# Hash bits on four column quarters and small placing transfers, in place of divisor sums on four column quarters, in an attention and feed-forward kernel

## The chip, the cores and the metric

The kernel runs on one core of a Trainium2 chip. The metric is device time in microseconds (us) of one execution. A core has engines that run side by side, each working through its own instructions in order: TensorE (PE, matrix products; PEld is its loading of weights), VectorE (DVE), ScalarE (ACT), GpSimd (POOL), and SyncE (SP), which here only issues DMA transfers. An instruction waits on semaphores until the work it needs is done; whatever stands behind it in the same queue waits too.

## The reference

Two stages. The first is attention with a hash mask, for 4 batches of 8 heads, 768 tokens, head size 64; the second is a feed-forward block on 3072 tokens of width 512 with 2048 hidden units.

```python
q_bits = (np.einsum('bhsd,dk->bhsk', q, proj) > 0)     # proj: 64 x 6
k_bits = (np.einsum('bhsd,dk->bhsk', k, proj) > 0)
q_bucket = np.sum(q_bits * powers, axis=-1)            # k_bucket alike
mask = q_bucket[:, :, :, None] == k_bucket[:, :, None, :]
scores = np.where(mask, scale * np.matmul(q, k.transpose(0, 1, 3, 2)), -1e9)
attn = softmax(scores)
out = np.matmul(attn, v)                               # to (B*S, H*D) = x
h = x @ w_in
g = h * erf(log1p(exp(h)))                             # a stable form of it
return g @ w_out
```

## The kernel before

**Attention.** Heads are taken two at a time: 16 pairs, heads a and b of a pair on partitions 0-63 and 64-127. A pair's 768 queries are cut into two halves of 384. So there are 32 half-pairs, numbered h, and half-pair h belongs to pair h // 2. For a half-pair, `score` (L529) computes six blocks of 128 keys x 384 queries for both heads into a PSUM tile `st`; the PSUM pool for such tiles (`big`) has three buffers. Each block takes two products: one in bf16 of the hash bits `kb` and `qb`, which adds a huge negative number wherever two buckets differ, and one in f32 of `k` and `q`. `exponential` (ACT, L543) takes the block to `e_all`, which holds nine blocks. `weigh` (L602) multiplies with `v` into `av`; `leave` (ACT, L659) copies `av` to the tile `x`, of which there are two buffers, one per pair.

**The hash bits.** `bits_of` (L358) multiplies q and k with `proj_sb` (128 x 64: six columns per head and zeros) for both halves of queries. `q` goes to partitions 0-63 and `k` to 64-127 of the PSUM tile, so two products run side by side on two column halves of the PE array. `sign_of` (ACT, L371) takes the sign of all 768 columns, `weigh_bits` (DVE, L382, once per head) multiplies the key's bits with weights into `kb`, `copy_bits` (DVE, L392) repeats the query's bits on partitions 64-127.

**The divisor.** `sum_keys` (DVE, L590) adds the six blocks of a half-pair in three or four instructions, most of them two blocks wide, in the memory of `x_sum` and of a block `x1` that the feed-forward part uses later. `divisor` (PE, L635) sums over the partitions with a 128 x 32 tile of ones, in four products of 192 columns on the four column quarters. `keep_divisor` (ACT, L648) copies the result to `z`. Per pair a chain through DRAM follows: `spread` (L678, `z` to `zd`), `gather` (L685, `zd` to `zc`, 12 numbers on each of 128 partitions), `invert` (DVE, L695 and L698), `ungather` (L703, to `rd`), `widen` (L713, two transfers, `rd` to `r` on all partitions), `normalise` (DVE, L721, `x` times `r`), and `send` (L727, `x` to `xs` in DRAM). `leave` of pair i writes the buffer of `x` that `send` of pair i-2 reads.

**Beside it.** `start_pair` issues the six loads of q, k and v (L342, L347; three sets of buffers). `measure` (ACT, L620) sums squares of q and k for a check of bounds. The 32 pieces of `w_in` and `w_out`, given as 64-bit floats, are fetched by POOL (L439) and turned to f32 by ACT (L453, L460) and DVE (L467 to L515); `presum_weights` (DVE, L742) makes sums of them.

**Order.** PE's order is written out by hand in `order`: after the first score, per half-pair h the scores of the next two quarters of work, then for even h the bits of the next pair, then the divisor of half-pair h-1, then the two `weigh`. All other instructions are placed by `arrange`, a list planner with a cost and a rank for each operation; it fixes the order on each engine, and the chip keeps to it. All transfers of the chain and all loads stand in one queue, SP's.

**Feed-forward.** The rest (L1098, L1238 on PE; L1116 to L1195 on ACT and DVE) uses Strassen-like sums of blocks, and is ordered by the same planner.

Of the kernel before, what the change touches and what calls it, by code (L numbers as in the profile page):

```python
# [63 lines left out]
P = 128  # L64
# [129 lines left out]
def kernel(  # L194
# [35 lines left out]
    QR = 32  # L230
    WARM = 7
    proj_sb = const.tile([P, 2 * QR], F32, name="proj_sb")
    weight = const.tile([P, 2], F32, name="weight")
    ones = const.tile([P, D], F32, name="ones")
# [23 lines left out]
    steps = const.tile([P, 5], F32, name="steps")  # L258
    for c, (end, factor) in enumerate(
        (  # L260
            (NBIT, NBIT + 1.0),
            (NBIT + 1, -float(NBIT)),
            (QR, -1.0),
            (QR + NBIT, NBIT + 1.0),
            (QR + NBIT + 1, -float(NBIT)),
        )
    ):
        nc.vector.tensor_scalar(
            out=steps[:, c : c + 1],
            in0=row,  # L270
            scalar1=float(end),
            scalar2=factor * BIG,
            op0=ALU.is_lt,
            op1=ALU.mult,
        )
    nc.vector.reduce_sum(out=weight[:, 0:1], in_=steps[:, 0:2], axis=AX.X)
    nc.vector.reduce_sum(out=weight[:, 1:2], in_=steps[:, 2:5], axis=AX.X)
    nc.vector.memset(sgn, -(2.0**-27))
# [87 lines left out]
    def sign_bits(d, bitp, cols):  # L366

        if cols.start == 0:
            for what in ("qb", "kb"):
                d[what] = bitp.tile([P, S], BF16, name=what, tag=what)  # L370
# [23 lines left out]
    def take_bits(d, bitp, halves=(0, 1)):  # L394
        cols = slice(halves[0] * HS, (halves[-1] + 1) * HS)
        sign_bits(d, bitp, cols)
# [4 lines left out]
    def attention():  # L401
        NS = NPAIR * 4
        with (
            tc.tile_pool(name="load", bufs=3) as load,
            tc.tile_pool(name="bitp", bufs=2) as bitp,
# [8 lines left out]
            def big(name):  # L414
                return psum.tile([P, 2, 512], F32, name=name, tag="big", bufs=3)

            junk = ep.tile([P, HS], BF16, name="junk")
            NE = 3 * GC
            e_all = ep.tile([P, NE, 2, HS + 1], F32, name="e_all")
            nc.vector.memset(e_all[:, :, :, HS : HS + 1], 1.0)  # L420
            pairs = {}
            raws = {}
            NH = NPAIR * 2
            wide_sums = [
                t.rearrange("p a b c -> p (a b c)")[:, 0 : 4 * HS].rearrange(
                    "p (n a c) -> p n a c", n=2, a=2
                )
                for t in (x_sum[:, :, :, :], blocks[1][:, :, :].rearrange("p k (a t) -> p k a t", a=2))
            ]
# [107 lines left out]
            def block(n, c):  # L537
                return e_all[:, (n * GC + c) % NE, :, :]
# [8 lines left out]
            def sum_steps(h):  # L547

                at = [(2 * h * GC + k) % NE for k in range(2 * GC)]
                if h >= NH - 2:
                    return [((0, 1), (0, 1), (1, 1), 0)] + [((k,), "s0", (k, 1), 0) for k in range(2, 6)]
                if at[3] == at[2] + 1:
                    return [
                        ((0, 1, 2, 3), (0, 2), (2, 2), 2),
                        ((4, 5), "s2", (4, 2), 2),
                        ((), "s0", "s1", 0),
                    ]
                return [  # L560
                    ((0, 1, 3, 4), (0, 2), (3, 2), 2),
                    ((2,), "s0", (2, 1), 0),
                    ((5,), "s1", (5, 1), 1),
                    ((), "s0", "s1", 0),
                ]

            def last_sum(h):
                return len(sum_steps(h)) - 1 if h >= 0 else 0

            def sum_keys(h, k):  # L570
                i, half = divmod(h, 2)
                d = pairs[i]
                if k == 0:
                    if h >= NH - 2:
                        d["sum", half] = sums.tile([P, 1, 2, HS], F32, name="sum", tag="sum")
                    else:
                        d["sum", half] = wide_sums[h % 2]
                s = d["sum", half]
                _, one, two, where = sum_steps(h)[k]

                def term(what):
                    if isinstance(what, str):
                        n = int(what[1])
                        return s[:, 0:2, :, :] if n == 2 else s[:, n : n + 1, :, :]
                    first, count = what
                    first = (2 * h * GC + first) % NE
                    return e_all[:, first : first + count, :, 0:HS]

                into = s[:, 0:2, :, :] if where == 2 else s[:, where : where + 1, :, :]
                nc.vector.tensor_tensor(out=into, in0=term(one), in1=term(two), op=ALU.add)  # L590
# [26 lines left out]
            def measure(i, n, half):  # L617
# [3 lines left out]
                    out=junk,  # L621
# [5 lines left out]
            def divisor(h):  # L627


                i, half = divmod(h, 2)  # L630
                d = pairs[i]
                z = d["z_ps"] = bank("z_ps")[:, 0 : HS // 2]
                for n in range(4):
                    ab, part = divmod(n, 2)
                    nc.tensor.matmul(  # L635
                        out=z[n * QR : (n + 1) * QR, :],
                        lhsT=ones[:, 0:QR],
                        rhs=d["sum", half][:, 0, ab, part * HS // 2 : (part + 1) * HS // 2],
# [3 lines left out]

            def keep_divisor(h):
                i, half = divmod(h, 2)
                d = pairs[i]
                if half == 0:
                    d["z"] = home(i, "z")
                nc.scalar.copy(  # L648
                    out=d["z"][:, half * HS // 2 : (half + 1) * HS // 2], in_=d.pop("z_ps")
                )  # L650
# [22 lines left out]
            def spread(i):  # L673

                d = pairs[i]
                zd = d["zd"] = dram.tile([2, 4, HS // 2], F32, name="zd", tag="zd")
                d["zc"] = small.tile([P, 2 * S // P], F32, name="zc", tag="zc")
                nc.sync.dma_start(  # L678
# [1000 lines left out]
```

## Time and profile before

| | us |
|---|---|
| median of three runs | 933.58 (931.9 to 934.86) |
| the profiled execution, its own time | 934.86 |
| its span, first to last instruction | 932.9 |
| attention, from the first score to the first product of the feed-forward part | 9.65 to 339.4 |
| PE busy in that stretch of 329.75 us | 325.91 |
| DVE, ACT busy in it | 300.17, 256.07 |
| PE busy after 339.4, in 593.5 us | 583.63 |

Between the profiled execution's own time and its span lie 2 us outside the instructions. Engine times are busy times; idle time of an engine costs something only where another engine waits for it in the end. The granted clock of PE is 0.997 of full speed.

### The profile page before, as it was taken

Reading aid. Unit: us, or ns where it says so; the run is one execution under the profiler, and the core shown is the slowest. Engines: PE = TensorE matmul, PEld = TensorE weight load, DVE = VectorE, ACT = ScalarE, POOL = GpSimd, SP = SyncE. Lnnn points to the kernel's source line nnn. Section 1 sums busy time; section 2 is a strip of 40 time slices with the busy share of each in tenths; the row PEclk is TensorE's granted clock in tenths of the full one; section 3 lists DMA queues with packets and bytes.
Section 4 is the critical chain, followed back from the end, with each engine's and each line's share of the span. In section 5 each row is a group of like instructions: output and inputs, shape, how many; then the busy total and the mean of one; then the engine's idle time right before and its main releaser. Section 6 shows DMA issues by size and latency. Waiting matters only on the chain.

```text
span 932.9 us, 12993 instructions
## 1 busy us (share of the span) xinstructions
PE 916.8 (98%) x5003; PEld 661.9 (71%) x5003; DVE 829.7 (89%) x1041; ACT 771.0 (83%) x1002; POOL 17.4 (2%) x35
## 2 busy tenths in 40 slices
PE   8999999999999999999999999999999999999996
PEld 3444444444444458888888888888888888888885
DVE  4999998999888997899999889998899789988995
ACT  5888787768876838999998998899989997899891
POOL 0000000000000000000000000000000000000000
PEclk9999999999999999999999999999999999999998
DMA  8365455576654322010212012210221111001211
GB/s 198 99 158 147 132 148 139 147 200 165 147 149 131 97 103 97 1 46 34 80 68 79 34 46 69 80 34 34 79 78 36 34 65 49 34 34 46 68 35 48
DMA packets 61398, 80.92 MB, mean 87 GB/s; under 512 B 33296, under 2 KB 46224, under 8 KB 61328
## 3 DMA queue, kind: packets, MB, share of 16 engines
q1 hardware_dynamic: 56672, 64.08, 23.9%
q0 software_dynamic: 4352, 15.73, 5.6%
q8 instruction: 41, 0.67, 0.3%
q10 hardware_dynamic: 304, 0.20, 0.1%
q14 instruction: 29, 0.24, 0.1%
HBM read 64.07 MB, written 15.93 MB: 86 GB/s over the span
## 4 chain that ended last, share of the span: by engine, by line
PE 85%; DVE 7%; DMA 4%; ACT 2%; issue 1%; SPq 0%; DVEq 0%; ACTq 0%
PE M L1238 30%; PE X L1098 27%; PE st L529 11%; PE av L602 9%; PE M L1098 3%; PE bits L358 2%; DMA xs<-x 1%; ACT e_all L543 1%; DVE x_sum L590 1%; PE z_ps L635 1%; DVE x L590 1%; DMA zd<-z 1%; DMA zc<-zd 1%; DVE x L721 1%; DMA r<-rd 1%
## 5 line engine op out<-in xcount | busy, mean ns | idle before, releaser
L1165 DVE SCALAR_TENSOR_TENSOR e<-w,e 128x1024 f32<-128x1024 f32 x144 | 173.4, 1221 | 5.8 <-ACT w L1161 3.0
L1161 ACT ACTIVATE w<-w,cq 128x1024 f32<-128x1024 f32 x144 | 160.7, 1143 | 1.9
L543 ACT ACTIVATE e_all<-st 128x768 f32<-128x768 f32 x192 | 149.1, 819 | 11.3 <-PE st L529 11.3
L529 PE MATMUL st<-q,k 64*128 64x384 f32 x768 | 156.6, 486 | 0.0
L1238 PE MATMUL M<-w_out_sb,h 128*128 128x256 f32 x576 | 140.2, 380 | 0.4 <-DVE h L1180 0.4
L602 PE MATMUL av<-e_all,v 128*64 128x385 f32 (+1 forms) x768 | 131.1, 490 | 0.0
L1098 PE MATMUL X<-x,w_in_sb 128*128 128x256 f32 x512 | 121.2, 380 | 0.0
L1238 PEld LDWEIGHTS M<-w_out_sb,h 128*128 128x128 f32 x576 | 109.3, 190 | 15.9 <-DVE h L1180 1.1
L1098 PEld LDWEIGHTS X<-x,w_in_sb 128*128 128x128 f32 x512 | 97.1, 190 | 13.8 <-ACT h L1116 0.6
L602 PEld LDWEIGHTS av<-e_all,v 128*64 128x64 f32 x768 | 52.4, 136 | 67.2 <-issue 65.4
L1238 PE MATMUL M<-wt,S 128*128 128x256 f32 x384 | 93.4, 379 | 0.4 <-DVE S L1195 0.4
L529 PEld LDWEIGHTS st<-q,k 64*128 64x128 f32 x768 | 69.1, 190 | 32.8 <-issue 32.1
L1098 PE MATMUL X<-x_sum,w_sum 128*128 128x256 f32 x344 | 81.7, 380 | 1.8 <-ACT h L1116 1.8
L1238 PEld LDWEIGHTS M<-wt,S 128*128 128x128 f32 x384 | 72.9, 190 | 10.7 <-DVE S L1195 0.8
L1098 PEld LDWEIGHTS X<-x_sum,w_sum 128*128 128x128 f32 x344 | 65.1, 190 | 12.0 <-ACT h L1116 3.3
L1116 ACT COPY h<-X 128x512 f32<-128x512 f32 x85 | 49.0, 577 | 22.3 <-PE X L1098 21.4
L1142 DVE SCALAR_TENSOR_TENSOR w<-w,e 128x1024 f32<-128x1024 f32 x48 | 58.4, 1221 | 9.6 <-ACT w L1137 9.3
L529 PE MATMUL st<-qb,kb 64*128 64x384 bf16 x384 | 63.7, 327 | 3.3 <-ACT e_all L543 3.2
L1180 DVE TENSOR_TENSOR h<-h,e 128x1024 f32<-128x1024 f32 x48 | 58.0, 1221 | 6.1 <-ACT e L1176 5.9
L659 ACT COPY x<-av 128x384 f32<-128x384 f32 x32 | 15.3, 478 | 57.4 <-DMA xs<-x 28.8
L1156 ACT ACTIVATE w<-e 128x1024 f32<-128x1024 f32 x48 | 50.4, 1050 | 13.3 <-DVE e L1152 13.0
L1152 DVE TENSOR_TENSOR e<-e,w 128x1024 f32<-128x1024 f32 x48 | 57.5, 1219 | 2.7 <-ACT e L1148 2.6
(117 smaller groups left out, 1421.0 us busy)
## 6 DMA issues: line engine op xcount, KB each, us to landing
wt<-wt SPq DMA_DIRECT2D x24, 768.0 KB, 4.3
raw<-in_w_out_dram POOLq DMA_DIRECT2D x16, 512.0 KB, 3.9
raw<-in_w_in_dram POOLq DMA_DIRECT2D x14, 512.0 KB, 4.2
v<-in_v_dram SPq DMA_DIRECT2D x32, 192.0 KB, 4.5
xs<-x SPq DMA_DIRECT2D x16, 384.0 KB, 2.4
q<-in_qkT_dram SPq DMA_DIRECT2D x30, 192.0 KB, 3.4
k<-in_qkT_dram SPq DMA_DIRECT2D x30, 192.0 KB, 4.2
r<-rd SPq DMA_DIRECT2D x30, 192.0 KB, 3.5
```

The source lines that it names most:

```text
L529: nc.tensor.matmul(out=st[:, ab, 0:HS], lhsT=d["k" + src][rows, keys], rhs=d["q" + src][rows, cols], start=(part == 0), stop=(part == 1),)
L543: nc.scalar.activation(out=e[:, :, 0:HS], in_=st[:, :, 0:HS], func=AF.Exp, scale=scale)
L602: nc.tensor.matmul(out=d["av"][rows, 0:w], lhsT=d["v"][:, g * GC + c, rows], rhs=e[:, ab, 0:w], start=(g == 0 and c == 0), stop=(g == 1 an ...
L1098: nc.tensor.matmul(out=d[where][:, u, :], lhsT=a[:, kc, f : f + P], rhs=b[:, kc, :], start=(first and u == 0 and kc == 0), stop=(last and ...
L1116: nc.scalar.copy(out=quarter(p, q), in_=st[p][where])
L1142: nc.vector.scalar_tensor_tensor(out=w, in0=w, scalar=-1.0, in1=st[p]["e", v], op0=ALU.add, op1=ALU.subtract)
L1152: nc.vector.tensor_tensor(out=s, in0=s, in1=st[p].pop(("w", v)), op=ALU.subtract)
L1156: nc.scalar.activation(out=z, in_=st[p]["s", v], func=AF.Square)
L1161: nc.scalar.activation(out=q, in_=z, func=AF.Square, bias=cq[:, j : j + 1])
L1165: nc.vector.scalar_tensor_tensor(out=s, in0=st[p].pop(("q", v, j)), scalar=ERF_Q[j][1], in1=s, op0=ALU.add, op1=ALU.mult,)
L1180: nc.vector.tensor_tensor(out=h, in0=h, in1=st[p].pop(("s", v)), op=ALU.mult)
L1238: nc.tensor.matmul(out=banks[name][:, sub, :], lhsT=a[:, u, sub * P : (sub + 1) * P], rhs=b[:, u, :], start=(c == 0 and k == 0), stop=(c = ...
```

## The change

Pairs 1 to 15 get their hash bits in another way; pair 0 keeps the old one. `bits_of` now multiplies with `proj_q` (128 x 32, head a in columns 0-5, head b in 16-21), and q and k of both halves of queries go to four column quarters of one PSUM bank. One `sign_of` of 384 columns makes a bf16 tile `sg` of them, one `weigh_bits` weighs the key's rows in place, and `place_bits` issues eight DMA transfers on SP, each of 7 rows of 384 bf16 numbers, from `sg` to the rows of `qb` and `kb` where they belong. Those two tiles exist twice (`spare`), filled with zeros by POOL beforehand; the set that pair 0 has used is cleared by `clean`. The bits of a pair come earlier in PE's order: pair 1's after the second quarter of scores, then after each odd half-pair's scores the bits of the pair after the next.

The sums over keys are single blocks again, five instructions of 128 x 768 a half-pair; `divisor` is two products of 384 columns on two column halves with 64 columns of ones; `keep_divisor` copies 384 columns; `spread` is two transfers of one row each. The nine blocks of exponentials are nine tiles, and `measure` writes its unused squares into `x_sum`, for which the first `presum_x` now waits. The feed-forward part is the same.

```diff
+    proj_q = const.tile([P, QR], F32, name="proj_q")
+    weight_q = const.tile([P, 1], F32, name="weight_q")
...
-    steps = const.tile([P, 5], F32, name="steps")
+    steps = const.tile([P, 8], F32, name="steps")
...
+            (QB, -1.0),
+            (QB + NBIT, NBIT + 1.0),
+            (QB + NBIT + 1, -float(NBIT)),
...
+    nc.vector.memset(proj_q, 0.0)
+    for ab in range(2):
+        rows = slice(ab * D, ab * D + D)
+        nc.vector.tensor_copy(
+            out=proj_q[rows, ab * QB : ab * QB + NBIT],
+            in_=proj_in[rows, ab * NBIT : (ab + 1) * NBIT],
+        )
+    nc.vector.reduce_sum(out=weight_q, in_=steps[:, 5:8], axis=AX.X)
+    nc.vector.tensor_tensor(out=weight_q, in0=weight_q, in1=weight[:, 0:1], op=ALU.add)
+    nc.vector.tensor_copy(out=weight_q[D + QR : P, :], in_=weight_q[D : D + QR, :])
...
-            e_all = ep.tile([P, NE, 2, HS + 1], F32, name="e_all")
+            sg = bitp.tile([P, HS], BF16, name="sg")
+            spare = {
+                (what, n): bitp.tile([P, S], BF16, name=f"{what}{n}")
+                for n in range(2)
+                for what in ("qb", "kb")
+            }
+            for what in ("qb", "kb"):
+                nc.gpsimd.memset(spare[what, 1], 0.0)
+            etiles = [ep.tile([P, 2, HS + 1], F32, name=f"e{n}") for n in range(3 * GC)]
...
+            def sum_keys(n, c):
+                d = pairs[n // 4]
+                key = "sum", n // 2 % 2
+                if n % 2 == 0 and c == 1:
+                    d[key] = sums.tile([P, 2, HS], F32, name="sum", tag="sum")
+                    before = block(n, 0)[:, :, 0:HS]
+                else:
+                    before = d[key]
+                nc.vector.tensor_tensor(
+                    out=d[key], in0=before, in1=block(n, c)[:, :, 0:HS], op=ALU.add
+                )
...
-                z = d["z_ps"] = bank("z_ps")[:, 0 : HS // 2]
-                for n in range(4):
-                    ab, part = divmod(n, 2)
+                z = d["z_ps"] = bank("z_ps")[:, 0:HS]
+                for ab in range(2):
                     nc.tensor.matmul(
-                        out=z[n * QR : (n + 1) * QR, :],
-                        lhsT=ones[:, 0:QR],
-                        rhs=d["sum", half][:, 0, ab, part * HS // 2 : (part + 1) * HS // 2],
+                        out=z[ab * D : ab * D + D, :],
+                        lhsT=ones,
+                        rhs=d["sum", half][:, ab, :],
...
-                nc.scalar.copy(
-                    out=d["z"][:, half * HS // 2 : (half + 1) * HS // 2], in_=d.pop("z_ps")
-                )
+                nc.scalar.copy(out=d["z"][:, half * HS : (half + 1) * HS], in_=d.pop("z_ps"))
...
-                nc.sync.dma_start(
-                    out=zd.rearrange("h n c -> n h c"),
-                    in_=d["z"][0 : 3 * QR + 1 : QR, 0:HS].rearrange("n (h c) -> n h c", h=2),
-                )
+                for ab in range(2):
+                    nc.sync.dma_start(out=zd[ab : ab + 1, :], in_=d["z"][ab * D : ab * D + 1, :])
...
             def bits_of(i):
-                hash_bits(pairs[i], big)
+                d = pairs[i]
+                d["bits"] = big("bits")
+                for n, what in enumerate("qk"):
+                    for half in range(2):
+                        row = (2 * n + half) * QR
+                        nc.tensor.matmul(
+                            out=d["bits"][row : row + QR, 0, 0:HS],
+                            lhsT=proj_q,
+                            rhs=d[what][:, half * HS : (half + 1) * HS],
+                            start=True,
+                            stop=True,
+                        )
 
             def sign_of(i):
-                sign_bits(pairs[i], bitp, slice(0, S))
-
-            def weigh_bits(i, ab):
-                spread_bits(pairs[i], slice(0, S), ab)
-
-            def copy_bits(i):
-                double_bits(pairs[i], slice(0, S))
+                nc.scalar.activation(
+                    out=sg,
+                    in_=pairs[i].pop("bits")[:, 0, 0:HS],
+                    func=AF.Sign,
+                    scale=2.0**100,
+                    bias=sgn[:, 0:1],
+                )
+
+            def weigh_bits(i):
+
+                nc.vector.tensor_scalar(
+                    out=sg[D:P, :],
+                    in0=sg[D:P, :],
+                    scalar1=weight_q[D:P, 0:1],
+                    scalar2=None,
+                    op0=ALU.mult,
+                )
+
+            def place_bits(i):
+
+                d = pairs[i]
+                for n, what in enumerate(("qb", "kb")):
+                    d[what] = spare[what, i % 2]
+                    for half in range(2):
+                        for ab in range(2):
+                            row = (2 * n + half) * QR + ab * QB
+                            nc.sync.dma_start(
+                                out=d[what][
+                                    ab * D : ab * D + NBIT + 1, half * HS : (half + 1) * HS
+                                ],
+                                in_=sg[row : row + NBIT + 1, :],
+                            )
+
+            def clean(n):
+
+                nc.gpsimd.memset(spare[("qb", "kb")[n], 0], 0.0)
...
-                if h % 2 == 0 and h // 2 + 1 < NPAIR:
-                    order.append(("bits", h // 2 + 1))
+                if h == 0:
+                    order.insert(2, ("bits", 1))
+                if h % 2 and (h + 3) // 2 < NPAIR:
+                    order.append(("bits", (h + 3) // 2))
```

## The prediction

> **What bounds the kernel now.** I read the windows first: between the first score (9.65 us) and the feed-forward part (339.4) PE is busy 325.91 of 329.75 us, DVE 300.17, ACT 256.07. So attention is a stream on PE with 3.84 us of holes, and DVE has little to spare. The feed-forward part keeps its instructions and their order; I give it no change. Next, one stage of a pair in PE's timeline, and the chain that ended last:
>
> ```profile
> 78.37 0.81 PE L529 MATMUL st<-q,k 64*128 64x384 f32 x4
> 79.11 0.54 PE L358 MATMUL bits<-q,proj_sb 128*64 128x384 f32 x1
> 79.11 0.54 PE L358 MATMUL bits<-k,proj_sb 128*64 128x384 f32 x1
> 79.48 0.49 PE L358 MATMUL bits<-q,proj_sb 128*64 128x384 f32 x1
> 79.49 0.49 PE L358 MATMUL bits<-k,proj_sb 128*64 128x384 f32 x1
> 79.81 0.49 PE L358 MATMUL bits<-q,proj_sb 128*64 128x384 f32 x1
> 79.81 0.49 PE L358 MATMUL bits<-k,proj_sb 128*64 128x384 f32 x1
> 80.13 0.49 PE L358 MATMUL bits<-q,proj_sb 128*64 128x384 f32 x1
> 80.13 0.49 PE L358 MATMUL bits<-k,proj_sb 128*64 128x384 f32 x1
> 80.55 0.53 PE L635 MATMUL z_ps<-x,ones 128*32 128x192 f32 x8
> 81.01 4.10 PE L602 MATMUL av<-e_all,v 128*64 128x385 f32 x24
> ```
> ```profile
> 69.74 0.46 PE z_ps L635 x8
> 70.20 4.02 PE av L602 x24
> 74.23 4.95 PE st L529 x36
> 79.18 1.44 PE bits L358 x8
> 80.62 0.46 PE z_ps L635 x8
> 81.08 4.03 PE av L602 x24
> ```
>
> The reader sees that each f32 product is two passes, that two column halves run at once (a pair of bits passes each 0.325 us), and that four quarters do too (eight passes of 192 columns in 0.46 us). A pair's stage is 2 x (4.95 + 0.46 + 4.03) + 1.44 = 20.3 us. Then the holes, from PE's timeline, and ACT's waits:
>
> ```profile
> 148.93 0.34 PE L529 MATMUL st<-qb,kb 64*128 64x384 bf16 x2 [0.32 <-ACT e_all L543]
> 211.13 0.34 PE L529 MATMUL st<-qb,kb 64*128 64x384 bf16 x2 [0.75 <-ACT e_all L543]
> 213.09 0.34 PE L529 MATMUL st<-qb,kb 64*128 64x384 bf16 x2 [0.17 <-ACT e_all L543]
> 294.94 0.34 PE L529 MATMUL st<-qb,kb 64*128 64x384 bf16 x2 [1.99 <-ACT e_all L543]
> ```
> ```profile
> 293.69 0.48 ACT L659 COPY x<-av 128x384 f32<-128x384 f32 x1 [5.99 <-DMA xs<-x]
> ```
> ```profile
> ACT x L659 <- DMA xs<-x: 28.8, 7, 6.0
> ```
>
> The holes are one mechanism: `leave` stands in ACT's queue until `send` of two pairs ago has landed, with the exponentials behind it. PE's weighted sum ended near 290.4, the copy began at 293.7, 3.3 us late, and PE lost 1.99. At 147.69 it was 1.6 late (PE lost 0.32), at 168.23 1.3 late (nothing). So a `send` costs PE about its lateness less 1.3 us. These holes sum to 3.2 us; the other 0.6 is at 339.
>
> **The change part by part.**
>
> *Bits on PE.* Four passes after another become two, of four quarters each: 1.44 - 2 x 0.325 = 0.79, a gain of 0.65 x 15 pairs = 9.75 us, all on the path. No row shows four quarters at 384 columns; the ends are 0 (no more overlap than now) and 9.75. I take 9.75, from the nearest row, the divisor's eight passes.
>
> That row meets a rule of the Trainium skill that speaks against the change: "TensorE: Matmul & The Clock Gate", Part 3 (packing small matmuls), measures three column tiles of width 32 at 2.38 times one, not 3. Scaled so, as an estimate, the gain would be 0.48 a pair, 7.2 us. Eight passes in 0.46 us leave no such loss, so I keep the row.
>
> *Divisor on PE.* Two products of 384 columns are two steps of 0.325 = 0.65, in the same shape as `av` right behind; before it was 0.46. Loss 0.19 x 32 = 6.1 us. If the 0.13 that the old form spends beyond 2 x 0.165 remains, it is 0.78 and 10.2 us. I take 6.1: bits of this shape show 0.32 from step to step.
>
> *DVE.* Sums: 134.1 us for 30 half-pairs before (L590 less the narrow last two), 4.47 each; five of 0.952 are 4.76: +8.7. Bits: two of 0.419 and one of 0.354, less one of 0.319 (64x384 row): -0.87 x 15 = -13.1. Net -4.4 us, nothing on the path while DVE's about 19 us a stage stay under PE's new 2 x (4.95 + 0.65 + 4.02) + 0.79 = 20.03. If that cover goes, divisors wait; the sums have some 5 us of slack before theirs.
>
> *ACT.* Signs 0.901 to 0.580, -4.8; divisor copies 0.312 to 0.478 (the 128x384 copy of L659), +5.3; covered, ACT is busy some 16 us in 20.
>
> *Start.* DVE gets about 1 us more (three 0.08 steps, two 0.17 copies, small ones); it was done at 4.8 and its weights are first used at 8.02. POOL's memsets have no row here; POOL is idle but for DMA issues until the second set of bits is placed near 20. `clean` waits for pair 0's last score, near 26, and holds weight fetches behind it: POOL's fetches wait 298 us in attention, this is hidden. Pair 1's bits now come after six score blocks, at 16.3. Its PSUM buffer must be free for the ninth block at 18.8, but ACT has three `measure` of 0.65 between exponential six (ended 17.26) and the sign: 19.2 + 0.58 = 19.8. A hole of 1.1 us (0 if those run earlier, 2 if later). Pair 1's loads are issued by 8.3 and land about 4.5 later: no wait.
>
> *SP's queue*, the open term. Per pair it gets eight placing DMAs and one more `spread`, and `send` now stands behind placing and behind the next pair's six loads. Let T be the start of a stage, T' the next, 20 us later. The divisor is out of PSUM near T+7 (six exponentials of 0.81, two copies, one square); two `spread` issues at most 0.58 each, landing 3.4 to 4.0 later (as now, behind loads): T+11.2; gather lands 2.2 to 2.7 after: T+13.7; invert 0.4, ungather 1.5, widen 1.28: T+17.1. The sign is done at T+16.7. Then eight issues: between 0.33 (`send`, `gather`) and 0.61 (`widen`) each. I take 0.60 with its gap, as `zd<-z` (0.58) also takes few partitions: T+21.9 = T'+1.9. Six loads 3.65: T'+5.5. `send` lands 2.4 later if alone, 5.5 if it drains behind the loads (an estimate: 3.5, as `spread` does now, and 2 for its own bytes): T'+7.9 to T'+11. `leave` is due at T'+9.6, and PE loses from T'+10.9. So in most pairs nothing. In four early pairs `presum_weights` (1.22 each) stands before invert in DVE's order, once in two and twice in two: T'+12.1 and T'+13.4 at worst, 2 x 1.2 + 2 x 2.5 = 7.4 us. Bounds 0 and 7.4; I take 2, since the late end needs every bound at once. The 3.2 us of now go, because `normalise` stands before T'+2 in DVE's order, where it now comes at T'+8. The loads themselves land near T'+10 and are first read at T'+14.6.
>
> A page that speaks against small transfers: "DMA: Bandwidth & Descriptors", rules for kernel authors, says that under 64 KB a transfer is mostly overhead, about 2.0 us each. Eight in series would be 16 us a stage and would move `send` past any slack. Here issues of 6 KB transfers take 0.33 to 0.58 and land in 1.4 to 2.2, and nothing waits between two of them, so only the issue counts.
>
> *Sum*: -9.75 + 6.1 + 1.1 - 3.2 + 2.0 = -3.75 us. Against the profiled execution's 934.86 (span 932.9 and 2 outside) that is 931.1; that execution is 1.3 above the median, so the forecast is 933.58 - 3.75 = 929.8.
>
> **The rivals.** All share -9.75 + 6.1 + 1.1 - 3.2 = -5.75 before new holes.
>
> *1. Holes vanish.* No `send` is late and the start costs nothing: -6.85, 926.7. For it: the low ends of the issue row. It counts with the forecast; together -6.85 to -2.8, times 926.7 to 930.8.
>
> *2. Some holes.* 3 to 8.5 us of them, of the four early pairs or of single late DMAs as at 289 (a landing of 4.2): within 0.3% of now, 2.8 us, which is about what a measurement of this kernel can tell. About 933.
>
> *3. `send` becomes the bound* (slower). Place: SP's queue, a pair's placing and loads ahead of `send`. At 0.69 an issue (0.61 and a gap of 0.08) and 5.5 to land it arrives at T'+11.8, 0.9 past T'+10.9: 0.9 x 13 pairs = 11.7, and the early pairs on top 7.4: 19.1, so 933.58 - 5.75 + 19.1 = 946.9. It decides when the holes exceed 5.75 us, 0.44 a pair; half of this price gives 937.4. Against it: 0.61 is the dearest issue row, and the landing behind loads is bound from above.
>
> *4. The quarters don't overlap at 384 columns*, the change does not do what it says: bits stay 1.44, +9.75: 939.6. Against it: the eight passes in 0.46.
>
> **How the numbers follow.** Forecast and rival 1: 0.47. Rival 2: 0.23. Rival 3: 0.18. Rival 4: 0.07; a wait that I don't see, slower: 0.05. So faster 0.47, same 0.23, slower 0.30. For 8 in 10 the range goes from 926, just under rival 1, to 942, past rival 4 and the middle of rival 3, leaving out rival 3's dear end. The forecast's own is 926.7 to 930.8.
>
> **What would show it.** In the profile after: bits of a pair near 0.8 us in the chain, divisors 0.65 to 0.7 with no gap to `av`; a hole near 18.8 on PE; `xs<-x` no longer first among ACT's waits; placing issues of 0.33 to 0.6. Wrong would be: bits at 1.4 (rival 4), ACT's `leave` waiting for `xs<-x` longer than 28.8 us with holes in most stages (rival 3), or PE waiting for placed bits or for the loads.

## The result, and the profile after

The changed kernel is slower: 958.15 us (954.01 to 963.1, four runs) against 932.96 (931.9 to 934.86, four runs of the kernel before beside them), a ratio of 1.027 with an interval of 1.0216 to 1.0324. The forecast was 929.8, in a range of 926 to 942. The profiled execution took 956.93 us, span 955.1; the feed-forward part begins at 362.10 instead of 339.38 us and takes 593.0 instead of 593.5. All of the loss is in attention.

PE's work came out as forecast. The chain of waits of the changed kernel (start, duration, engine and line), in its last undisturbed stage:

```profile
320.01 0.78 PE bits L754 x8
320.80 0.80 PE z_ps L616 x4
321.59 3.87 PE av L585 x24
325.46 4.95 PE st L545 x36
330.41 0.80 PE z_ps L616 x4
331.21 3.88 PE av L585 x24
```

Bits 0.78 instead of 1.44; divisor and `av` together 4.67 instead of 4.49. A stage of PE's work is 2 x (4.95 + 4.67) + 0.78 = 20.02 us. But stages took 22.4 us in the mean (twelve of them lie between the placings that begin at 53.95 and at 322.46 us), and PE stood still in most of them. Two rows of the summary of waits (line waited at, by whom released: us in total, times, longest):

```profile
ACT x L637 <- DMA xs<-x: 66.0, 12, 6.5
PE st L545 <- ACT e L559: 23.7, 13, 2.8
```

ACT's copy `leave` waited 66.0 us for a `send` to land, before 28.8. One such place in ACT's timeline, and what PE lost by it in PE's (in brackets the idle time before and its releaser):

```profile
157.25 0.48 ACT L637 COPY x<-av 128x384 f32<-128x384 f32 x1 [5.12 <-DMA xs<-x]
```
```profile
158.49 0.34 PE L545 MATMUL st<-qb,kb 64*128 64x384 bf16 x2 [1.83 <-ACT e L559]
```

Why that `send` was late is in SP's timeline of the same stage, whose T' (the end of PE's last `weigh`) is 144.44:

```profile
142.54 3.10 SPq L789 DMA_DIRECT2D qb<-sg  x4
145.74 2.90 SPq L789 DMA_DIRECT2D kb<-sg  x4
148.74 1.16 SPq L358 DMA_DIRECT2D q<-in_qkT_dram  x2
149.95 1.22 SPq L358 DMA_DIRECT2D k<-in_qkT_dram  x2
151.27 1.30 SPq L363 DMA_DIRECT2D v<-in_v_dram  x2
152.69 0.48 SPq L700 DMA_DIRECT2D xs<-x  x1
153.26 0.59 SPq L657 DMA_DIRECT2D zd<-z  x2
157.13 0.35 SPq L661 DMA_DIRECT2D zc<-zd  x1
160.12 0.34 SPq L677 DMA_DIRECT2D rd<-zc  x1
161.70 2.22 SPq L686 DMA_DIRECT2D r<-rd  x2
```

Eight placing issues took 6.1 us, 0.76 each with the gap. `send` was issued at T' + 8.25 and landed 4.5 us later, at T' + 12.7. Read as a sum, the queue spends 14.3 us a stage issuing and 7.2 standing at landings (3.3 at `zd`, 2.6 at `zc` and `invert`, 1.2 at `rd`): 21.5, more than PE's 20.0. In 11 of 13 stages the placing began within 0.2 us of the end of `widen`, so the queue itself held it back there.

Something else slowed PE, that the forecast did not have. Two windows of 20 us (busy times of PE, PEld, DVE, ACT, POOL; then the granted clock, DMA share, GB/s), and PE's timeline in the second:

```profile
120.00:140.00 20.00, 17.14 (x118) 8.12 (x116) 17.48 (x27) 12.94 (x23) 1.06 (x2) 1.00 0.55 140
200.00:220.00 20.00, 17.31 (x110) 7.98 (x108) 16.14 (x24) 16.19 (x29) 1.05 (x2) 0.91 0.49 161
```
```profile
203.29 0.51 PE L545 MATMUL st<-qb,kb 64*128 64x384 bf16 x2 [2.69 <-ACT e L559]
203.57 1.51 PE L545 MATMUL st<-q,k 64*128 64x384 f32 x4
```

The windows 200 to 220, 240 to 260 and 280 to 300 hold 0.91 of the clock; before, attention had 1.00 throughout. In each of the three PE runs slowly for a while behind a hole (2.69, 2.81 and 2.00 us long): the three blocks of scores up to the bits take 3.90, 4.22 and 4.22 us, where they take 2.53 behind the holes at 158.49 and 227.19. That is 4.8 us. A hole of 2.78 us at 136.21, in the first window above, left the clock at 1.00, so what decides it is not shown. The ledger of the 22.7 us by which attention became longer, profile against profile: bits -0.66 x 15 = -9.9, divisor +0.18 x 32 = +5.8, the start +0.68, the old holes -3.2, the new holes +23.7; that is 17.1. With the slow stretches it is 21.9; the last 0.8 us were not taken apart.

### The profile page after: what moved, and what is told of

It is laid out like the page before. It is cut to its first block, busy times and chain, and to the rows that moved or that the text cites. A ratio compares the mean times of both kernels' runs of the same rounds, so it can differ in the third digit from the quotient of the medians.

```text
span 955.1 us, 13091 instructions
## 1 busy us (share of the span) xinstructions
PE 918.6 (96%) x4875; PEld 664.3 (70%) x4875; DVE 827.5 (87%) x1078; ACT 769.0 (81%) x1002; POOL 19.8 (2%) x39
## 4 chain that ended last, share of the span: by engine, by line
PE 69%; DVE 14%; DMA 8%; ACT 3%; issue 2%; SPq 2%; DVEq 0%; ACTq 0%
PE M L1254 30%; PE X L1114 27%; DVE sum L571 7%; PE st L545 5%; DMA xs<-x 4%; PE av L585 4%; PE M L1114 3%; ACT e L559 2%; DMA zd<-z 2%; SPq L358 1%; DMA zc<-zd 1%; PE z_ps L616 1%; DVE top L483 1%; DVE x L694 1%; DVE rest L523 1%
## 5 line engine op out<-in xcount | busy, mean ns | idle before, releaser
L545 PE MATMUL st<-q,k 64*128 64x384 f32 x768 | 160.2, 495 | 0.0
L559 ACT ACTIVATE e<-st 128x768 f32<-128x768 f32 x192 | 147.1, 824 | 7.6 <-PE st L545 7.1
L571 DVE TENSOR_TENSOR sum<-sum,e 128x768 f32<-128x768 f32 x128 | 121.6, 950 | 13.5 <-ACT e L559 4.9
L585 PE MATMUL av<-e,v 128*64 128x385 f32 (+1 forms) x768 | 129.5, 486 | 0.0
L585 PEld LDWEIGHTS av<-e,v 128*64 128x64 f32 x768 | 55.0, 137 | 69.0 <-issue 67.4
L545 PEld LDWEIGHTS st<-q,k 64*128 64x128 f32 x768 | 71.1, 194 | 30.2 <-issue 28.8
L545 PE MATMUL st<-qb,kb 64*128 64x384 bf16 x384 | 65.2, 333 | 24.4 <-ACT e L559 23.7
L1254 PEld LDWEIGHTS M<-wt,S 128*128 128x128 f32 x384 | 72.9, 190 | 10.7 <-DVE S L1211 0.8
L545 PEld LDWEIGHTS <-kb 64*128 64x128 bf16 x384 | 22.7, 95 | 73.7 <-issue 46.4
```

The source lines that it names most:

```text
L545: nc.tensor.matmul(out=st[:, ab, 0:HS], lhsT=d["k" + src][rows, keys], rhs=d["q" + src][rows, cols], start=(part == 0), stop=(part == 1),)
L559: nc.scalar.activation(out=e[:, :, 0:HS], in_=st[:, :, 0:HS], func=AF.Exp, scale=scale)
L571: nc.vector.tensor_tensor(out=d[key], in0=before, in1=block(n, c)[:, :, 0:HS], op=ALU.add)
L585: nc.tensor.matmul(out=d["av"][rows, 0:w], lhsT=d["v"][:, g * GC + c, rows], rhs=e[:, ab, 0:w], start=(g == 0 and c == 0), stop=(g == 1 an ...
L1254: nc.tensor.matmul(out=banks[name][:, sub, :], lhsT=a[:, u, sub * P : (sub + 1) * P], rhs=b[:, u, :], start=(c == 0 and k == 0), stop=(c = ...
```

## Experiments: the placing off SP, first of it, fewer of it, twice

Theory S says that SP's queue sets the stage. Its first test keeps all the work and PE's order, and issues the eight placing transfers from POOL (the planner moves a few instructions of ACT and DVE):

```diff
-                            nc.sync.dma_start(
+                            nc.gpsimd.dma_start(
...
-                        "SP",
-                        2.7,
+                        "POOL",
+                        8.0,
```

> The eight placing transfers of a pair are issued by POOL instead of SP; everything else as in the changed kernel. Theory S (SP's queue is the loop that sets the stage: placing 6.2 us of issue, loads 3.9, send 0.6, spread 0.6 and 3.9 to land, gather with invert some 4, ungather 1.5, widen 1.1, together about 22 us a pair against PE's 20.03): the loop falls to about 16 us, the holes of PE in front of the scores (24.4 us) shrink under 3, and the time is 928 to 934. Rival D (DVE: five single-block sums a half-pair make divisors and normalise late): no change, 953 to 960. Rival C (the small transfers slow the other transfers on the DMA engines, so that a send lands in 4.5 instead of 2.4 us): the same transfers still run, so little change, 950 to 960.

928.0 us (925.87 to 929.52), 0.9951 of the kernel before, interval 0.9933 to 0.9969. In SP's timeline `send` is again early (xs at 138.38, right behind the loads) and the queue has idle time before and behind it:

```profile
134.07 1.19 SPq L358 DMA_DIRECT2D q<-in_qkT_dram  x2
135.30 1.23 SPq L358 DMA_DIRECT2D k<-in_qkT_dram  x2
136.63 1.12 SPq L363 DMA_DIRECT2D v<-in_v_dram  x2
138.38 0.34 SPq L700 DMA_DIRECT2D xs<-x  x1
142.14 0.55 SPq L657 DMA_DIRECT2D zd<-z  x2
```

The holes are gone, ACT's waits for `send` are down from 66.0 us to one of 2.7, the granted clock is 1.00 in all of attention, and the feed-forward part begins at 332.69: 6.7 us before 339.38, where the terms without new holes say 6.6. So the loss comes in with the placing on SP's queue. DVE's single sums (rival D) and the small transfers as such (rival C) are still there, and are out as its cause. Two more runs change how much of it there is. Half as many transfers, of 14 rows:

```diff
-    QB = QR // 2
+    QB = proj2.shape[1] // 2 + 1
...
-                        for ab in range(2):
-                            row = (2 * n + half) * QR + ab * QB
...
+                            out=d[what][D - QB : D + QB, half * HS : (half + 1) * HS],
+                            in_=sg[row : row + 2 * QB, :],
```

> Head b's bits stand right behind head a's in a quarter (rows 7 to 13), and the bit rows of the two heads stand side by side on partitions 57 to 70 of qb and kb, so that one transfer of 14 rows replaces two of 7: four issues a pair instead of eight, the same bytes. Theory S: an issue costs the same 0.70 us and a gap, so SP's loop loses 3.1 us, to about 19 us, just under PE's 20.03; holes fall from 24.4 to 2 to 8 us, time 930 to 939. Rival D: 953 to 960. Rival C, if it goes by bytes or rows: 950 to 960.

940.67 us (938.23 to 944.15), 1.0087, interval 1.0054 to 1.012, just above the 930 to 939 of theory S. An issue of 14 rows took 0.75 to 0.79 us in the median, so a pair's placing fell from 6.1 to 3.4, the waits for `send` to 50.8 us and PE's holes from 23.7 to 11.7. And each transfer twice (`for again in range(2):` around the issue):

> Each placing transfer is issued twice in a row, 16 a pair. Theory S: SP's loop grows by 8 x 0.75 = 6 us to about 28 us a pair, and the stage with it: 956.9 + 6 x 13 = 1030 to 1040. Rival D: up to 965. Rival O: the send is 6 us later in each stage, which gives the same 1030 to 1040; this run tells S and O from D only.

1212.35 us, in one run. The direction fits, the size does not: sixteen issues took some 24 us and not 12, because each repeated write waited on SP for the landing of the first (waits for `qb` and `kb` of 92.0 and 86.3 us in total). The run says little more about S. The third keeps all transfers and lets `start_pair` wait for `send`, so that `send` stands ahead of the loads (`("send", i - 4)` added to what `start_pair` waits for):

> The loads of pair i wait, in the planner, for the send of pair i-4, so that send stands ahead of the six loads in SP's queue, as it did in the kernel before; nothing is removed. Theory S (length of the loop): the same issues and landings stand in series, so SP falls behind by 1 to 2 us a stage until something else waits; holes stay above 12 us, time 943 to 958. Rival O (only the place of send behind the loads costs, not the length of the queue): holes vanish, 928 to 934.

950.68 us, in one run, in which the planner also ordered ACT and DVE otherwise. PE's waits for the exponentials are fewer (14.5 us in 9), but from one placing to the next it is still 22.0 us in the mean (ten stages from 96.09 us). Sending ahead of the loads, but behind the placing, is no cure.

## Experiments: each half of the change alone, and the loads off SP

Only the sums and the divisor of the change, with the bits of before:

> The kernel before with only the second half of the change: sums one block at a time on separate tiles, a two-column-half divisor, `spread` as two transfers; the hash bits and their signs stay as they were, on VectorE. TensorE's terms of the prediction give +0.19 us for each of 32 divisors: 932.0 + 6.1 = 938.1 us (937 to 940), if `SP` has room for one more 0.6 us issue per pair, which its idle time before `send` in the kernel before says. Rival (the queue was already at its edge, so any one issue more makes holes): over 941. Rival (the divisor's extra time is hidden): 932 to 934.

936.21 us, 1.0059, interval 1.0045 to 1.0073: +5.8 over the 930.38 beside it, where PE's term says +6.1. Only the bits of the change, with the sums of before, placed on SP and then on POOL:

> The kernel before with only the first half of the change: bits on column quarters, one sign, eight placing transfers on `SP`; wide sums, quarter divisor and `spread` as one transfer stay as before. Theory S (the serial loop of the `SP` queue sets the stage): the loop loses one issue of 0.6 us against the changed kernel's 22.4, so 21.8 a stage against TensorE's 19.7; the time is set by the loop as in the kernel with four transfers (21.6 a stage, 940.7): 938 to 946 us, although TensorE has 6.1 us less work than in the changed kernel. Rival P (TensorE's terms simply add to the holes): 958.2 - 6.1 = 952 us. Rival (the placing is harmless by itself and it is the sums that fall behind): 921 to 928.

> As the kernel with only the new bits, but the eight placing transfers go out on the `POOL` queue. Theory S and TensorE's terms together: the changed kernel with its placing on `POOL` took 928.0; without the wider divisor's 0.19 x 32 = 6.1 us it takes 921.9 (920 to 924), which is below the kernel before by the bits' 9.75 us and the old holes, less the start. Rival (the sums in separate tiles are needed for the earlier signs, so the wide sums hold TensorE up now that it is faster): 924 to 930.

954.53 us (ratio 1.0258, 1.0233 to 1.0282) and 919.71 us (0.9884, 0.9869 to 0.9898). The second is the fastest kernel of this study, 10.7 us under the one before. The first is a miss for S as it was put: with one issue less the queue should have come to 21.8 us a stage and 938 to 946 us. It lost nearly as much as the whole change, though PE has less work; part of that is the clock, 0.97 in its attention against 0.99 in the changed kernel's. Its placings between 118 and 186 us begin 21.4 to 24.5 us apart: a shorter sum of issues did not make a shorter stage. The next run says this more clearly. It leaves the placing on SP and issues the six loads from POOL:

```diff
-                queue = nc.scalar if quick and what == "k" and half == 0 else nc.sync
+                queue = nc.scalar if quick and what == "k" and half == 0 else nc.sync if quick else nc.gpsimd
```

> The changed kernel, its placing transfers left on `SP` at their 6.1 us a pair, but the six loads of a pair (3.7 us of issues) go out on the `POOL` queue. Theory S (it is the sum of the issues in one queue, not the placing transfers as such): the loop falls from 22.4 to 18.7 us, below TensorE's 20.0, and the time to that of the placing on `POOL`: 926 to 932 us. Rival T (the transfers that place the bits are themselves slow or disturb others, wherever the rest is issued): 945 to 958.

953.78 us (1.025, 1.0226 to 1.0274). S fails here: 3.7 us of issues left the queue and the stages still took 22 to 24 us. SP's waits (line waited at, releaser: total, times, longest):

```profile
SPq L677 <- DVE zc L672: 94.7, 16, 8.2
SPq L686 <- DMA rd<-zc: 67.5, 16, 6.0
```

In the changed kernel these were 52.4 and 24.1. The loads now ran while the divisor's round trip did, and its landings took the time that the issues had left free. Rival T has the number right.

## Experiments: two links, cut one at a time and together

What S lacks is the second half of the picture: `leave` waits for `send`, and the queue's loop stands at landings. First a third buffer for `x`, so that `leave` no longer waits:

```diff
+                if what == "x" and i % 3 == 2 and i < NPAIR - 4:
+                    return x_sum.rearrange("p a k t -> p (a k t)")[:, S : 2 * S]
```

> The changed kernel with a third buffer for `x` (every third pair keeps its x in a part of x_sum that is idle in this stage, up to pair 11), so that `leave` no longer waits for the `send` of two pairs before, which lands late behind the loads. Everything on the queues stays. Theory L (the late send is the link that makes the holes: 66 us of ACT's waits before `x` are waits for it, and it is 21% of the chain between 120 and 190 us): the holes go and the time falls to 926 to 934 us, as with the placing on `POOL`. Theory S2 (the in-order queue as a closed loop: placing 6.2 us, loads 3.9, send, spread, then standing at the landing of zd, of zc with `invert`, of rd, then widening, and only behind it the next placing; 21.5 to 22.4 us whatever `leave` does): 945 to 957 us, with the waits for xs gone from ACT and the same interval from one placing to the next.

951.24 us (1.0216, 1.0185 to 1.0247), as S2 says. With the waits for `send` gone, the next thing that comes late behind the placing can end PE's wait, the loads that the next bits need. They end 4.3 of 14.1 us of PE's waits; the rest is spread over others. From the chain of this kernel:

```profile
168.42 0.69 SPq L791
169.22 0.53 SPq L358
169.79 0.60 SPq L358
170.43 0.59 SPq L358
171.06 5.32 DMA k<-in_qkT_dram
176.51 0.84 PE bits L756 x4
```

Then the round trip and `send` on POOL, which cuts the loop in two:

> The changed kernel with the divisor's round trip (spread, gather, ungather, widen) and `send` on the `POOL` queue, between the raw weights; the placing and the loads stay on `SP`, in the same order. Theory S2 (the loop is closed because one in-order queue holds both the placing and the landings that it must stand at): cut in two, `SP` holds 10.2 us of issues a stage and no landing, and the time is TensorE's: 926 to 932 us. Theory U (transfers that run beside one another land late, as with the loads on `POOL`, where rd and r took 5 to 6 us to land; here the round trip can fall beside the loads as well): 940 to 956 us, with landings of rd and r over 4 us.

949.42 us (1.0183, 1.015 to 1.0216): a miss for S2. SP now has time in hand, but `send` is early in some stages only, and behind it on POOL stands a piece of weights and then `spread`, which lands late. From the chain:

```profile
147.53 1.02 DVE x L694
148.83 0.58 POOL xs L700
149.41 0.54 POOL raw L455
149.95 0.49 POOL zd L657
150.44 5.12 DMA zd<-z
```

T' was 142.65 there: `normalise` began at T' + 4.9, `send` was issued at T' + 6.2, and the copy of `leave` began at T' + 10.4, just in time. In other stages it was not: a `send` issued at 191.71 let `leave` go at 199.20, and PE lost 5.12 us. Both cuts together, and the changed kernel without the reciprocal's three steps:

> Two links cut at once in the changed kernel: the round trip and send on the POOL queue (as in the last kernel but one, 949.4), and a third buffer for x (as in the one before it, 951.2). Theory S3 (there are two links, either of which alone holds the stage above 20 us: the SP queue's closed loop of issues and landings, and the send that lands after TensorE's half stage, so that each cut alone leaves the other): with both cut 926 to 934 us. Rival M (the loss is spread over many small lateness terms, landings and DVE's order among them): 938 to 948 us.

> The changed kernel without gather, invert and ungather: z is widened straight from where spread put it, so x is multiplied by the divisor instead of its reciprocal (the reciprocal is left out; the rest is as before). On SP this takes out two issues of 0.35 us and the standing at zc's landing, invert and rd's landing, some 6 us of the 21.5 to 22.4. Placing, loads and send keep their place and price. Theory S3: the queue's loop falls to some 16 us, it has time in hand again, placing, loads and send all go out earlier: 924 to 932 us. Rival T (the placing transfers themselves, or send behind them, cost TensorE the time, however long the rest of the queue takes): 942 to 958 us.

With both links cut: 942.61 us (1.0124, 1.0093 to 1.0155). PE's holes fell to 7.8 us, the start's among them, and the feed-forward part begins at 342.73, so of the 29.4 us of attention that lie between the changed kernel and the one with the placing on POOL, 19.4 came back; the total missed S3's range, partly because the feed-forward part was 3 us longer. Without the reciprocal: 951.03 us (1.021, 1.0176 to 1.0245), a miss for S3. Its queue did have time in hand, but did not use it to place earlier, for the placing waits for the signs, which PE's order fixes. SP's timeline of it (nothing is issued from the end of widening at 137.0 to the placing):

```profile
135.93 1.10 SPq L673 DMA_DIRECT2D r<-zd  x2
141.79 3.21 SPq L776 DMA_DIRECT2D qb<-sg  x4
145.05 2.89 SPq L776 DMA_DIRECT2D kb<-sg  x4
148.05 1.16 SPq L358 DMA_DIRECT2D q<-in_qkT_dram  x2
149.25 1.30 SPq L358 DMA_DIRECT2D k<-in_qkT_dram  x2
150.65 1.12 SPq L363 DMA_DIRECT2D v<-in_v_dram  x2
151.86 0.49 SPq L687 DMA_DIRECT2D xs<-x  x1
```

So the length of the loop isn't needed for most of the loss: PE's waits for the exponentials still come to 17.6 us, against 23.7 in the changed kernel. Released when the signs are ready, the placing stands ahead of the loads and of `send` every time, and `send` lands 5.4 us after 151.86, too late.

## Experiments: the same transfers at another place in the queue

That leaves the place. Three runs moved the placing behind `send` by giving the planner other dependences:

> The changed kernel with the same eight placing transfers on the same SP queue, but at another place in it: q's four go behind the loads and send of their stage, k's four between gather and ungather, in time in which the queue stood at zc's landing and at invert. The placed bits aren't read before the next stage begins, some 20 us later. Theory Q (the price a placing costs is not what hurts, but that its 6.2 us stand ahead of the loads and of send, which the half stage waits for, and add to a loop that stands at landings in between): the loop is 14.3 us of issues, 3.3 at zd, 1.3 at rd and 0.6 left at zc, 19.5 us, just below TensorE's 20.03; send lands before T' + 9.6: 926 to 936 us. Rival R (7-row transfers on this queue cost the stage their time wherever they stand): 945 to 958 us.

> The changed kernel with all eight placing transfers between gather and ungather; send goes ahead of the loads. Theory Q: the queue stood 3.7 us there, so the placing costs the round trip 2.5 us more and the loop is 18.9 us; normalise and send come some 2.5 us later than with the split, which is near send's due time: 926 to 940 us, at or above the split. Rival R: 945 to 958 us.

> The kernel before with only the new bits (wide sums and the quarter divisor kept), placed on SP as in the split. Theory Q: the 919.7 us of the same bits placed on the POOL queue, or a little above: 918 to 926 us. Rival R: the 954.5 us of the bits placed on SP ahead of the loads: 945 to 956 us.

946.11 us (1.0152, 1.0107 to 1.0197), 995.89 us (1.069, 1.0658 to 1.0721) and 943.2 us (1.012, 1.0086 to 1.0154), all misses, for two reasons of my own making. I had written that the bits are needed a stage after the placing; PE's order has the next pair's first scores ahead of the current pair's last `weigh`, some 14 us after T'. In the run with all of the placing late PE waits for it in most stages (15 waits, 38.4 us; first fence, its timeline), and the clock in its attention is 0.93. And the planner, given other dependences, put both of ACT's conversions of a weight piece ahead of the exponential that the bits wait for (second fence, the split).

```profile
126.11 0.51 PE L545 MATMUL st<-qb,kb 64*128 64x384 bf16 x2 [3.13 <-DMA kb<-sg]
```
```profile
116.75 0.52 PE L754 MATMUL bits<-q,proj_q 128*32 128x384 f32 x2 [0.33 <-ACT e L559]
```

So two more runs moved nothing but the issues. The planner sees the changed kernel; `place_bits` only notes what is to be placed, and q's transfers are issued after those of `send`, k's after those of `spread`. PE, ACT, DVE and POOL keep every instruction in its place.

```diff
             def place_bits(i):
+                waiting.extend((i, n) for n in range(2))
...
                 nc.sync.dma_start(out=xs[b][j], in_=pairs.pop(i)["x"])
+                place_next()
...
                     nc.sync.dma_start(out=zd[ab : ab + 1, :], in_=d["z"][ab * D : ab * D + 1, :])
+                place_next()
```

> The changed kernel with every instruction of PE, ACT, DVE and POOL in the same order as in it, and the same transfers on SP; only their place in the SP queue differs: q's four placing transfers behind the loads and send, k's four behind spread. The two runs before moved the placing too late for TensorE (the bits are read some 14 us after the stage begins, kb landed up to 3.9 us after that) and changed ACT's order (0.5 us before the bits in each stage); this one does neither. Theory Q: send goes out 6.2 us earlier and lands before T' + 9.6; zd's landing is spent placing k; the loop is 14.3 + 3.7 at zc + 1.3 at rd = 19.3 us, under TensorE's 20.03: 926 to 934 us. If the loop of the queue can't be brought under the stage that way (rd, zc or the loads late by a microsecond a stage): 938 to 946. Rival R (these transfers on SP cost the stage wherever they stand): 946 to 958 us.

> The kernel with only the new bits (wide sums and quarter divisor kept; 954.5 us with the placing on SP ahead of the loads, 919.7 on POOL), every engine but SP in the same order as the first of these, q's placing behind the loads and send, k's behind spread. Theory Q: TensorE's stage is 19.66 us here and the queue's loop 18.7 to 19.3: 918 to 928 us. Rival R: 943 to 955 us.

The changed kernel so: 935.65 us (1.0054, 1.0033 to 1.0076), just above the 926 to 934 of theory Q and far from R's 946 to 958. The bits alone so: 925.88 us (0.9938, 0.9916 to 0.9959), within Q's range and faster than before. The same eight transfers, in the same queue, at the same 0.7 us each. SP's timeline of the first of them, and ACT's waits for `send` in it:

```profile
136.65 1.18 SPq L358 DMA_DIRECT2D q<-in_qkT_dram  x2
137.87 1.23 SPq L358 DMA_DIRECT2D k<-in_qkT_dram  x2
139.20 1.12 SPq L363 DMA_DIRECT2D v<-in_v_dram  x2
140.57 0.34 SPq L703 DMA_DIRECT2D xs<-x  x1
141.01 3.06 SPq L804 DMA_DIRECT2D qb<-sg  x4
144.98 1.45 SPq L659 DMA_DIRECT2D zd<-z  x2
146.88 3.12 SPq L804 DMA_DIRECT2D kb<-sg  x4
150.11 0.37 SPq L664 DMA_DIRECT2D zc<-zd  x1
```
```profile
ACT x L639 <- DMA xs<-x: 9.1, 3, 3.7
```

After the start PE's holes in attention come to 5.0 us, 3.15 of it in one place. ACT waits 9.1 us for `send`, not 66.0. Of the 30.2 us between the changed kernel (958.15) and the placing on POOL (928.0), 22.5 are gone by the place in the queue alone; of the 34.8 between the two kernels with the bits alone, 28.7. What keeps the last 6 to 8 us was not taken apart: single late stages (the hole of 3.15, a wait for `kb`, with a clock of 0.96 in its 40 us) are part of it.

## Why the prediction was wrong

*Bits on PE: right.* 0.65 a pair was predicted, 0.66 measured; four quarters overlap fully at 384 columns. The estimate from the Trainium skill's "TensorE: Matmul & The Clock Gate", Part 3, (0.48) was not borne out. The kernel with the bits alone, placed on POOL, gained 10.7 us. Rival 4 is out.

*Divisor: right.* 0.18 against 0.19 a half-pair, +5.8 against +6.1.

*DVE, ACT: covered, as predicted;* no hole on PE ended with DVE's sums.

*Start: overstated.* 0.68 us against 1.1.

*Old holes: a weak base.* The 3.2 us were real in the profiled execution, but that took 934.86, and the kernel before had medians of 930.4 to 932.1 in the later comparisons. (The profiled execution with only the new divisor took 935.23, hardly more, although the medians lie 5.8 apart.) Such a term should be taken off the execution that shows it, and less of it off a median.

*SP's queue: the step that failed.* The path was the right one, down to "a `send` costs PE about its lateness less 1.3 us": landing at T' + 12.7 against T' + 9.6 gives 3.1 - 1.3 = 1.8, and the hole was 1.83. The sizes up to the issue of `send` were wrong, all to one side:

| | predicted | measured in the stage shown |
|---|---|---|
| placing begins | T' - 2.9 | T' - 1.9 |
| eight issues | 4.8 (0.60 each with the gap) | 6.1 (0.76) |
| placing ends | T' + 1.9 | T' + 4.2 |
| loads issued | T' + 5.5 | T' + 8.1 |
| `send` lands | T' + 7.9 to T' + 11 | T' + 12.7 |

The price of the placing issue was taken from `zd<-z` at 0.58, and 0.61 was called the dearest issue row; rival 3 was set aside on that ground. But no row of before shows a transfer from one on-chip tile to another of few partitions, so nothing bounded it from above. At 0.76 an issue, and with the late end of the landing, the same working gives T' + 12.4, 1.5 us of loss in each of 13 pairs, 19.5 us, and 933.58 - 5.75 + 19.5 = 947.3: rival 3, which is what happened. So the price, together with the late end that the forecast had not taken, is 17.5 of the 28.4 us by which it missed. That T' + 12.4 comes so near to the measured 12.7 is in part luck: the placing began 1.0 us later than forecast, and the landing took 4.5 us, not 5.5. The run without the reciprocal shows the price by itself. Its placing began at T' - 3.7 (T' is 145.50 in the stage of its fence), earlier than forecast, and `send` landed at T' + 11.8 all the same; with 4.8 us for the eight issues it would have been T' + 10.5 (an estimate), before PE loses.

The rest of the miss: new holes were bound at 7.4 us, from four early pairs, but 12 of the copies of `leave` waited for `send`. I had added up a chain from T to T' with the landings in it and never closed it; the queue's loop (21.5 us) is longer than PE's stage (20.0). And the slow stretches behind holes, 4.8 us, were in no case. The Trainium skill's "DMA: Bandwidth & Descriptors" (Anatomy of one DMA) gives about 2.0 us as the fixed part of a transfer issued from GpSimd, most of it the wait for the landing. The estimate made from it, 16 us a stage for eight in series, is further from the 6.1 measured than the forecast's 4.8, though on the side of the result.

*What the runs add.* Neither the price nor the length of the queue alone is the cause. With the price unchanged and the placing behind `send`, three quarters of the loss goes. It was the eight issues' place, at this price, ahead of two things with early due times, the loads and `send`. Each link cut alone (third `x`, `send` ahead of loads, round trip elsewhere, reciprocal left out) left 949 to 951 us.

## What to carry to other kernels

Cheap transfers in an in-order queue cost what stands behind them: list for each issue ahead of others when its data are read and when the next ones' are, and put the one with slack last. Add up the queue's own loop, issues and the landings that it stands at, and hold it against the stage of the bound engine. Where an issue's form has no row in the trace, its price has no upper bound there either; and a link cut alone that brings nothing doesn't acquit the queue, for the next link may be just as late.

## What the runs showed of the hardware that I had not expected

- An issue of 7 rows x 384 bf16 from tile to tile took 0.69 to 0.70 us on SP in the median of the changed kernel; 14 rows took 0.75 to 0.79. On POOL four 7-row issues took 1.98 to 2.30 us, 0.50 to 0.58 each. `send`, 384 KB from 128 partitions, took 0.34 with the placing on POOL and 0.48 in the changed kernel.
- The granted clock can fall behind holes of 2.0 to 2.8 us: it was 0.91 in three windows of 20 us, but 1.00 behind a hole of 2.78 and, in the kernel before, behind one of 1.99. In the run with doubled transfers, with a hole of some 17 us a stage, it was 0.76 to 0.78 over 120 us, and PE's own work slowed with it. Such a hole costs more than its length.
- In this program a repeated write to the same rows stands in its queue until the first has landed, up to 3.5 us a time: eight more transfers a pair cost 18 us, not 6.
- Moving the loads to another queue let them run beside the divisor's round trip, and the queue's waits for one landing of 6 KB (`rd<-zc`) rose from 1.5 to 4.2 us in the mean, 6.0 at the longest.
